# Attention followed by a gated FFN on one core: another instruction order, other engines for some steps, and e buffers handed out as they come free

## The chip, the core and the metric

The program runs on one NeuronCore of a Trainium2 chip. Times are microseconds of device time of one execution. Five engines matter: TensorE (PE) for matmuls and transpositions, VectorE (DVE), ScalarE (ACT) and GpSimd (POOL) for everything elementwise, and SyncE (SP), which issues the DMAs. Each engine runs its own instructions in order and waits on semaphores for the others.

## The reference

```python
for c in range(nc):                       # chunks of 32 queries
    q_c = q[:, :, c_start:c_end]          # context: 16 keys to the left, 8 to the right
    k_full = np.concatenate([mem_k, k_ctx], axis=2)      # 8 memory keys + context
    v_full = np.concatenate([mem_v, v_ctx], axis=2)
    scores = scale * np.matmul(q_c, k_full.transpose(0, 1, 3, 2))
    a = np.exp(scores - np.max(scores, axis=-1, keepdims=True))
    a = a / (np.sum(a, axis=-1, keepdims=True) + 1e-09)
    out[:, :, c_start:c_end] = np.matmul(a, v_full)
...
h = np.maximum(x @ w_in, 0.0)             # 512 -> 1024
conv_out = sum(conv_w[k] * hp[:, k:k+S] for k in range(3))   # depthwise over the sequence
gate = 1.0 / (1.0 + np.exp(-conv_out))
return h * gate @ w_out                   # 1024 -> 512
```

There are 4 batches, 8 heads of 64, 768 positions; x is the attention's output with the heads side by side (512 channels). q, k, v are float32; w_in, conv_w and w_out are float64 and come to the chip as pairs of 32-bit words.

## The kernel before

**Attention.** The work is cut into steps: one step is a pair of heads (128 rows of channels) and half of a sequence, 12 chunks of 32 queries. The first four steps stand alone, the others go two by two (GROUP). `scores` (L310, PE) writes a step's scores into the tile s, a pair of PSUM banks of which there is one. The softmax follows: a maximum (L267, DVE), then by the letter in SOFT either V, a subtraction out of s into the SBUF tile e (L269, DVE) and one exp over e (L270, ACT), or A, a scaling of the maxima (L272, DVE) and one exp for each group of 64 columns straight out of s (L283, ACT: 6 for a single step, 12 for a pair). Then come a memset at the sequence's ends (L286, L288), a sum (L290), a reciprocal (L293), and a multiplication (L294) on DVE or POOL by the letter in NORM. PE transposes e (L325) into the tile t, ACT copies it to w_t (L327), PE multiplies with v (L334, into t again), and t is split into a high part x_hi (L340, ACT) and the rest x_lo (L341, DVE), so that matmuls in fp32r keep the precision of float32. There are one t, one w_t and two e, and before the change e is handed out strictly in turn.

**Weights.** Each of 8 blocks of w_in and of w_out is loaded as 512 KB of words (L208; conv_w with L210) into one of four buffers and turned from float64 into a high and a low part by `from_f64` (L212 to L240): some ten elementwise operations, whose spread over DVE, ACT and POOL is set by a letter (C, M, R, S, r) in W_IN and W_OUT.

**FFN.** `ffn_in` multiplies x by one 128-column block of w_in, for half a sequence: four channel blocks, for each three matmuls (high by high, high by low, low by high; L358) into one of four PSUM banks f, then relu on ACT (L366). `gate` runs over a whole sequence: a first tap on ACT (L374) or DVE (L376) by TAP, two multiply-adds on DVE (L378), sigmoid on ACT (L379), a product (L381, DVE or POOL by MULT). `split` makes the high (L387, ACT) and the low part (L388, DVE or POOL by LO). `ffn_out` multiplies 128 positions by w_out: eight blocks of three matmuls (L402) into a bank f, a copy (L405, ACT), a DMA out (L406).

**Order.** The functions record some 1300 operations in a Plan; `Plan.run` emits them in the order of the table ORDER, which sets the order on each engine; semaphores follow from the data. The batches interleave: while PE does the FFN of one batch, the attention of the next is worked off between its matmuls. A tile is made at its first use; a ring of n tiles must have the tile n places back finished by then. The loads stand in the same order on SP, and an SP instruction that waits for a buffer holds back the loads behind it.

Of the kernel before, what the change touches and what calls it, by code (L numbers as in the profile page):

```python
# [24 lines left out]
W_IN, W_OUT = ('CSSRMSCr', 'CMCRRSRM')  # L25
TAP = 'AAAAAAAAVAVAVVVAVAVAVVAAVVAAVVAV'
MULT = 'VVVGVVGVVVVVGGGVGVVVVGVVVGGGVVVV'
LO = 'VVVVGGGVVVVVVVVVGVVVGVVVVGVVGVGV'
SOFT = 'VVVVVAAVVAVBVVVBVBVVVAVVVVAVVBAA'
NORM = 'GGVGGGVVGGGGGVGGVVGGVVVVVVVGVGVG'  # L30
# [71 lines left out]
class Plan:  # L102

    def __init__(self):
        self.ops, self.last, self.readers = ([], {}, defaultdict(list))
        self.rings, self.parts = ({}, defaultdict(list))
# [434 lines left out]
```

## Time and profile before

| | us |
|---|---|
| median of 3 runs (lowest, highest) | 353.03 (352.73, 353.37) |
| profiled execution | 352.37 |
| its span | 350.6 |
| PE busy in the span | 334.1 (95%) |
| DVE busy | 233.1 (66%) |
| ACT busy | 191.9 (55%) |
| POOL busy | 83.6 (24%) |
| end of the last matmul | 347.4 |

The span lasts from the first to the last instruction of the profiled execution; 1.77 us of that execution lie around it. PE's matmuls are pipelined, so the duration of one is longer than the distance to the next: for pace, the starts are to be compared. PE's instructions come to its queue in blocks by a DMA queue of their own (q8, "instruction": 35 packets, 0.57 MB in the whole span, for all engines), beside the loads (q1).

### The profile page before, as it was taken

The numbers are of one execution on the slowest core, as the hardware profiler recorded it, in microseconds if no ns is written. First come the engines' busy times: TensorE is split into PE (matmuls) and PEld (weight loads), VectorE is DVE, ScalarE is ACT, GpSimd is POOL, SyncE is SP. The second block draws the span as 40 slices with busy tenths as digits, with TensorE's granted clock in tenths as the row PEclk, the third lists the DMA queues.
The fourth block names the chain that finished last, engine by engine and source line by source line (L and its number), as shares of the span: only waits on it lengthen the run. The fifth ranks groups of instructions, "written<-read, shape, count | busy, mean of one in ns | idle before, by whom it ended". The sixth has DMA issues, their size and how long they took to land.

```text
span 350.6 us, 10290 instructions
## 1 busy us (share of the span) xinstructions
PE 334.1 (95%) x4536; PEld 297.1 (85%) x4536; DVE 233.1 (66%) x325; ACT 191.9 (55%) x314; POOL 83.6 (24%) x127
## 2 busy tenths in 40 slices
PE   1589999999999999999999999999999999999996
PEld 0468999989999998887888999998888988998885
DVE  4977998999989997989974143286840332678300
ACT  4434785877687869379842323456743352545311
POOL 1464245124473154111020000402200012121200
PEclk9999999999999999999999999999999999999999
DMA  7966979667677244022401600001212000100022
GB/s 261 391 216 204 314 249 333 230 208 228 200 206 251 66 154 148 27 93 75 125 20 36 243 0 32 0 2 60 65 45 93 30 1 2 60 0 2 0 105 76
DMA packets 19916, 42.49 MB, mean 121 GB/s; under 512 B 2336, under 2 KB 10784, under 8 KB 19872
## 3 DMA queue, kind: packets, MB, share of 16 engines
q1 hardware_dynamic: 19872, 41.85, 35.6%
q8 instruction: 35, 0.57, 0.7%
q14 instruction: 9, 0.07, 0.1%
HBM read 35.55 MB, written 6.29 MB: 119 GB/s over the span
## 4 chain that ended last, share of the span: by engine, by line
PE 85%; DVE 9%; DMA 3%; issue 1%; ACT 0%; POOL 0%; DVEq 0%; ACTq 0%; POOLq 0%
PE f L402 38%; PE f L358 34%; PE t L334 6%; PE s L310 4%; PE t L325 3%; DMA w<-in_w_out_dram 2%; DVE c L378 1%; DMA w<-in_w_in_dram 1%; DVE w_top L217 1%; DVE e L269 1%; DVE top L267 1%; DVE w_top L214 1%; DVE w L223 1%; DVE w_top L216 1%; DVE w L221 1%
## 5 line engine op out<-in xcount | busy, mean ns | idle before, releaser
L402 PE MATMUL f<-w_out_hi,g 128*128 128x512 f32 (+1 forms) x400 | 127.3, 387 | 0.0
L358 PE MATMUL f<-x_hi,w_in_hi 128*128 128x384 f32 x256 | 90.3, 353 | 0.0
L402 PEld LDWEIGHTS f<-w_out_hi,g 128*128 128x128 f32 x400 | 74.1, 188 | 15.2 <-ACT o_sb L405 0.2
L358 PE MATMUL f<-x_lo,w_in_hi 128*128 128x384 f32 x256 | 86.7, 339 | 0.0
L358 PE MATMUL f<-x_hi,w_in_lo 128*128 128x384 f32 x256 | 86.7, 339 | 0.0
L402 PE MATMUL f<-w_out_lo,g 128*128 128x512 f32 (+1 forms) x200 | 77.0, 385 | 0.0
L378 DVE SCALAR_TENSOR_TENSOR c<-h,cw,c 128x768 f32<-128x768 f32 x48 | 49.2, 1044 | 18.6 <-ACT c L374 17.4
L358 PEld LDWEIGHTS f<-x_hi,w_in_hi 128*128 128x128 f32 x256 | 48.6, 190 | 2.7 <-issue 0.2
L358 PEld LDWEIGHTS f<-x_hi,w_in_lo 128*128 128x128 f32 x256 | 48.8, 190 | 1.0
L358 PEld LDWEIGHTS f<-x_lo,w_in_hi 128*128 128x128 f32 x256 | 48.5, 190 | 0.0
L402 PEld LDWEIGHTS f<-w_out_lo,g 128*128 128x128 f32 x200 | 37.6, 188 | 6.6
L405 ACT COPY o_sb<-f 128x512 f32<-128x512 f32 (+1 forms) x25 | 14.2, 573 | 43.4 <-PE f L402 41.3
L379 ACT ACTIVATE c<-c 128x768 f32<-128x768 f32 x32 | 26.9, 847 | 19.6 <-DVE c L378 19.5
L366 ACT ACTIVATE h<-f 128x384 f32<-128x384 f32 x48 | 22.6, 490 | 26.3 <-PE f L358 26.3
L388 POOL TENSOR_TENSOR g<-c,g 128x768 fp32r<-128x768 f32 x8 | 15.4, 1925 | 70.9 <-PE f L402 35.2
L334 PEld LDWEIGHTS t<-w_t,v_t 64*64 64x64 f32 x1536 | 25.2, 140 | 4.6 <-issue 3.3
L334 PE MATMUL t<-w_t,v_t 64*64 64x32 f32 x1536 | 27.2, 224 | 0.1
L387 ACT CAST g<-c 128x768 fp32r<-128x768 f32 x24 | 19.8, 833 | 12.6 <-POOL c L381 7.1
L376 DVE TENSOR_SCALAR c<-h,cw 128x768 f32<-128x768 f32 x14 | 8.6, 617 | 26.3 <-ACT h L366 23.6
L388 DVE TENSOR_TENSOR g<-c,g 128x768 fp32r<-128x768 f32 x16 | 17.3, 1086 | 11.2 <-ACT g L387 11.0
L381 POOL TENSOR_TENSOR c<-c,h 128x768 f32<-128x768 f32 x5 | 8.9, 1781 | 63.4 <-ACT c L379 63.4
L341 DVE TENSOR_TENSOR x_lo<-t,x_hi 128x768 fp32r<-128x768 f32 (+1 forms) x18 | 15.5, 859 | 12.6 <-ACT x_hi L340 12.6
(68 smaller groups left out, 408.5 us busy)
## 6 DMA issues: line engine op xcount, KB each, us to landing
v_t<-in_v_dram SPq DMA_DIRECT2D x32, 384.0 KB, 4.4
k_t<-in_k_dram SPq DMA_DIRECT2D x28, 252.0 KB, 3.9
out_dram<-o_sb SPq DMA_DIRECT2D x23, 256.0 KB, 2.0
q_d<-in_q_dram SPq DMA_DIRECT2D x28, 192.0 KB, 4.4
w<-in_w_in_dram SPq DMA_DIRECT2D x8, 512.0 KB, 6.2
w<-in_w_out_dram SPq DMA_DIRECT2D x8, 512.0 KB, 5.3
h<-in_k_dram SPq DMA_DIRECT2D x4, 252.0 KB, 6.1
h<-in_q_dram SPq DMA_DIRECT2D x4, 192.0 KB, 5.8
```

The source lines that it names most:

```text
L310: nc.tensor.matmul(s.t[w * CH:(w + 1) * CH, h ^ w & 1, (i * NG + g) * KW:(i * NG + g + 1) * KW], lhsT=q_d.t[r, c], rhs=k_t.t[r, c * STEP:c ...
L325: nc.tensor.transpose(out=t.t[:, j, g * P:(g + 1) * P], in_=e.t[:, i, 1:1 + 2 * KW], identity=ident)
L334: nc.tensor.matmul(t.t[h * D:(h + 1) * D, c & 1, c // 2 * CH:(c // 2 + 1) * CH], lhsT=vs[i].t[r, o], rhs=w_t.t[r, i, o], start=True, stop= ...
L341: plan.op(lambda: nc.vector.tensor_tensor(out=lo(), in0=sums(), in1=hi().bitcast(F32), op=ALU.subtract), (t, *keys(x_hi)), keys(x_lo))
L358: nc.tensor.matmul(f.t[:, :TW], lhsT=w_in_p[c][:, fc, cc], rhs=x_p[a].t[:, cc], start=cc == 0 and i == 0, stop=cc == NCC - 1 and i == 2)
L366: nc.scalar.activation(h.t[:, 1 + o:1 + o + TW], f.t[:, :TW], AF.Relu)
L378: plan.op(lambda i=i: nc.vector.scalar_tensor_tensor(out=c.t, in0=h.t[:, i:i + S], scalar=w[i], in1=c.t, op0=ALU.mult, op1=ALU.add), (*H, ...
L379: plan.op(lambda: nc.scalar.activation(c.t, c.t, AF.Sigmoid), (c,), (c,))
L387: plan.op(lambda: nc.scalar.copy(out=g_hi(), in_=x()), (h,), (p[0],))
L388: plan.op(lambda: (nc.vector if lo == 'V' else nc.gpsimd).tensor_tensor(out=g_lo(), in0=x(), in1=g_hi().bitcast(F32), op=ALU.subtract), (h ...
L402: nc.tensor.matmul(ps.t[:, :n], lhsT=g[fc][a].t[:, tt * P:(tt + 1) * P], rhs=w_out_p[c][:, fc, o:o + n], start=fc == 0 and i == 0, stop=fc ...
L405: plan.op(lambda: nc.scalar.copy(out=o_sb.t[:, :n], in_=ps.t[:, :n]), (ps,), (o_sb,))
```

## The change

Three things change. The strings that set engines are other ones: of the first four steps' softmax letters, VVVV becomes AVAA; the w_in and w_out blocks have other conversion letters; TAP has 19 letters A in place of 18; SOFT as a whole has as many or more steps by A, and MULT, LO and NORM differ in places. ORDER is another permutation (of 1305 operations, since the kinds of conversion have different numbers of operations). And the rings are counted by tiles that are alive instead of by turn, with the two e buffers handed out from a list to which a finished tile's buffer returns. Lines behind the top of the file move by 3 (in `from_f64` by 4).

```diff
-W_IN, W_OUT = ('CSSRMSCr', 'CMCRRSRM')
-TAP = 'AAAAAAAAVAVAVVVAVAVAVVAAVVAAVVAV'
-MULT = 'VVVGVVGVVVVVGGGVGVVVVGVVVGGGVVVV'
-LO = 'VVVVGGGVVVVVVVVVGVVVGVVVVGVVGVGV'
-SOFT = 'VVVVVAAVVAVBVVVBVBVVVAVVVVAVVBAA'
-NORM = 'GGVGGGVVGGGGGVGGVVGGVVVVVVVGVGVG'
+W_IN, W_OUT = ('MSSSCSMR', 'SMCRSRSM')
+TAP = 'AAAAAAAAVVAVAAAAVAVAVVAVAAVVAVVV'
+MULT = 'GVVGVVGVGVVVGVGVVVVVGVVVGVGVVGGV'
+LO = 'VVGGVVGVGVVVGVVVVVVGVVVVGVGVVVGV'
+SOFT = 'AVAAVAVVAAABVVVBVBVVAAVVVVVVVBVA'
+NORM = 'GGVGGGGVVGGGGVVGGVGGGVGVGVVGGGVG'
 ORDER = (
-    64, 65, 1, 0, 3, 75, 17, 16, 85, 70, 33, 32, 66, 67, 18, 68, 69, 2, 71, 72, 73, 74, 4, 76, 190, 49, 5, 6, 19, 77,
+    64, 1, 0, 74, 16, 17, 84, 70, 65, 2, 71, 33, 32, 66, 67, 68, 69, 72, 48, 3, 73, 4, 136, 75, 5, 49, 6, 76, 34, 77,
...
-        self.rings, self.parts = ({}, defaultdict(list))
+        self.rings, self.parts, self.freed = ({}, defaultdict(list), {})
...
-                    assert len(used) < size or not used[-size].left, i
+                    assert sum((y.left > 0 for y in used)) < size, i
...
             do()
+            for x in tiles:
+                if not x.left and x.ring in self.freed:
+                    self.freed[x.ring].append(x.t)
             done.add(i)
...
+    plan.ring('e', len(e_of))
+    plan.freed['e'] = e_of
...
-        plan.ring('e', len(e_of))
-        e = Tile('e', lambda: e_of[len(plan.rings['e'][1]) % len(e_of)])
+        e = Tile('e', lambda: plan.freed['e'].pop(0))
```

**DVE at the first softmax.** L217 to L224 are conversions of the first w_in block, L267 and L269 the first step's softmax (tile s in, e_71 out), L286 to L293 the rest of it. Before:

```order
L223 SCALAR_TENSOR_TENSOR w_80<-w_80 128x512
L224 TENSOR_SCALAR w_80<-w_top 128x512
L267 TENSOR_REDUCE top<-s 128x2x3
L269 TENSOR_TENSOR e_71<-s,top 128x2x3x64
L214 TENSOR_SCALAR w_top<-w_top 128x512
L216 TENSOR_SCALAR w_top<-w_top 128x512
L286 MEMSET e_71 32x2x16
L290 TENSOR_REDUCE z<-e_71 128x6
L293 RECIPROCAL z<-z 128x6
```

After (all lines 3 or 4 higher, so L270 is the maximum):

```order
L228 TENSOR_SCALAR w_80<-w_top 128x512
L236 SCALAR_TENSOR_TENSOR w_in_lo<-w_80 128x512
L270 TENSOR_REDUCE top<-s 128x2x3
L275 TENSOR_SCALAR top<-top 128x6
L218 TENSOR_SCALAR w_top<-w_top 128x512
L220 TENSOR_SCALAR w_top<-w_top 128x512
L221 SCALAR_TENSOR_TENSOR w_top<-w_86,w_top 128x512
L289 MEMSET e_71 32x2x16
L293 TENSOR_REDUCE z<-e_71 128x6
```

One conversion more (L236) stands ahead of the maximum, a scaling (L275) takes the subtraction's place, and the exps that follow it stand on ACT (six of L286, straight out of s).

**PE when it begins with the FFN.** t_276 (t_285 after) is the values' tile of the second step, s_359 (s_378) the scores of the first pair of steps, f the FFN's banks. Before:

```order
L334 MATMUL t_276<-w_t_311,v_t_128 64x32 x24
L358 MATMUL f_346<-x_hi0_270,w_in_hi_75 128x384
L358 MATMUL f_346<-x_hi0_270,w_in_lo_76 128x384
L358 MATMUL f_346<-x_lo0_273,w_in_hi_75 128x384
L310 MATMUL s_359<-k_t_234,q_d_181 32x64 x24
L310 MATMUL s_359<-k_t_187,q_d_142 32x64 x24
L358 MATMUL f_411<-x_hi0_270,w_in_hi_75 128x384
L358 MATMUL f_411<-x_hi0_270,w_in_lo_76 128x384
```

After:

```order
L337 MATMUL t_285<-w_t_322,v_t_185 64x32 x24
L361 MATMUL f_365<-x_hi0_265,w_in_hi_75 128x384
L361 MATMUL f_365<-x_hi0_265,w_in_lo_76 128x384
L361 MATMUL f_365<-x_lo0_274,w_in_hi_75 128x384
L313 MATMUL s_378<-k_t_292,q_d_289 32x64 x24
L328 MATMUL t_409<-ident_66,e0_71 128x128 x3
L361 MATMUL f_416<-x_hi0_265,w_in_hi_75 128x384
L361 MATMUL f_416<-x_hi0_265,w_in_lo_76 128x384
L361 MATMUL f_416<-x_lo0_274,w_in_hi_75 128x384
L313 MATMUL s_378<-k_t_272,q_d_276 32x64 x24
L337 MATMUL t_409<-w_t_422,v_t_153 64x32 x24
```

Before, both halves of the pair's scores stand together after the first triple of FFN matmuls. After, a transposition and a triple stand between them.

**SP ahead of the first w_out block.** The names are the loads' buffers and sources, and brackets give the engines and queues for which SP waits. Before:

```order
L301 DMA k_t<-in_k_dram 128x504 [waits DMAHW5_49,DMAHW2_49,PE_49]
L301 DMA k_t<-in_k_dram 128x504 [waits DMAHW6_49,DMAHW3_49,PE_49]
L301 DMA q_d<-in_q_dram 128x384 [waits DMAHW4_49]
L208 DMA w_902<-in_w_out_dram 128x1024 [waits DVE_49]
L301 DMA q_d<-in_q_dram 128x384
L208 DMA w_999<-in_w_out_dram 128x1024 [waits DMAHW7_49,Pool_49]
L301 DMA v_t<-in_v_dram 128x768 [waits DMAHW0_49]
L208 DMA w_1003<-in_w_out_dram 128x1024 [waits DMAHW1_49,Activation_49,Pool_49]
```

After:

```order
L304 DMA v_t<-in_v_dram 128x768 [waits DMAHW2_49,PE_49]
L304 DMA q_d<-in_q_dram 128x384 [waits DMAHW5_49,DMAHW3_49,PE_49]
L304 DMA q_d<-in_q_dram 128x384 [waits DMAHW6_49,DMAHW4_49,PE_49]
L304 DMA k_t<-in_k_dram 128x504
L212 DMA w_904<-in_w_out_dram 128x1024 [waits Pool_49]
L212 DMA w_910<-in_w_out_dram 128x1024 [waits DMAHW7_49,Pool_49]
L304 DMA k_t<-in_k_dram 128x504 [waits DMAHW0_49]
```

The load of the first w_out block waits for DVE before, and for POOL after the change; the second one follows it directly.

## Rows read from the trace of the kernel before

**Rows 1.** Parts 1 and 4 of the page: busy us of each engine (share of the span, instructions), and the shares of the chain of work that ended last by engine.

```profile
PE 334.1 (95%) x4536; PEld 297.1 (85%) x4536; DVE 233.1 (66%) x325; ACT 191.9 (55%) x314; POOL 83.6 (24%) x127
...
PE 85%; DVE 9%; DMA 3%; issue 1%; ACT 0%; POOL 0%; DVEq 0%; ACTq 0%; POOLq 0%
```

**Rows 2.** The waits of PE: who was waited for, us in total, times, the longest. First in the window from 0 to 27 us, then, behind the dots, in the window from 27 to 347 us.

```profile
PE s L310 <- DMA h<-in_q_dram: 8.3, 2, 6.8
PE t L325 <- POOL e L294: 3.2, 2, 1.6
PE s L310 <- issue: 1.5, 1, 1.5
...
PE t L325 <- DVE x_lo L341: 0.2, 1, 0.2
```

**Rows 3.** The table of stretches: the stretch, its length, busy us of each engine (instructions), the granted clock of PE, the busy share of the DMA engines and GB/s.

```profile
10.00:20.00 10.00, 6.73 (x210) 5.11 (x197) 9.65 (x25) 4.34 (x9) 4.74 (x5) 1.00 1.03 394
20.00:30.00 10.00, 8.49 (x179) 7.20 (x175) 6.14 (x13) 3.56 (x8) 5.60 (x5) 1.00 0.62 192
30.00:71.00 41.00, 41.00 (x985) 37.76 (x983) 38.12 (x66) 29.19 (x57) 16.21 (x26) 1.00 0.79 263
```

**Rows 4.** The timeline of all engines at the end of the program: start, duration, engine, line and operation.

```profile
347.49 0.37 ACT L405 COPY o_sb<-f 128x256 f32<-128x256 f32 x1 [1.55 <-PE f L402]
```

**Rows 5.** The timeline of all engines, 7 to 12 us, the first softmax and the second scores; in brackets the idle time ahead and what ended it.

```profile
7.84 0.56 DVE L267 TENSOR_REDUCE top<-s 128x6 f32<-128x384 f32 x1
...
8.51 0.56 DVE L269 TENSOR_TENSOR e<-s,top 128x384 f32<-128x384 f32 x1
...
9.10 0.53 ACT L270 ACTIVATE e<-e 128x384 f32<-128x384 f32 x1 [0.39 <-DVE e L269]
...
9.30 0.96 PE L310 MATMUL s<-h 64*32 64x64 f32 x48 [1.50 <-DMA h<-in_q_dram]
...
11.65 0.33 SPq L301 DMA_DIRECT2D k_t<-in_k_dram  x1
...
11.90 0.47 PE L325 MATMUL t<-ident,e 128*128 128x128 f32 x1 [1.65 <-POOL e L294]
```

**Rows 6.** Groups by line and form in the window from 0 to 80 us, of DVE and, behind the last dots, of ACT: line, engine, operation, tiles, shapes, count, busy us, mean ns of one.

```profile
L232 DVE SCALAR_TENSOR_TENSOR w_in_lo<-w 128x512 fp32r<-128x512 uint32 x1 | 0.7, 703 | 0.0
...
L272 DVE TENSOR_SCALAR top<-top 128x12 f32<-128x12 f32 x1 | 0.2, 168 | 0.0
...
L283 ACT ACTIVATE e<-s,top 128x64 f32<-128x64 f32 x12 | 2.6, 346 | 0.0
```

**Rows 7.** The timeline of PE from 16.5 to 28.5 us.

```profile
16.83 0.91 PE L325 MATMUL t<-ident,e 128*128 128x128 f32 x3 [1.55 <-POOL e L294]
...
21.56 0.97 PE L310 MATMUL s<-k_t,q_d 64*32 64x64 f32 x48
24.04 0.96 PE L310 MATMUL s<-k_t,q_d 64*32 64x64 f32 x48 [1.51 <-issue]
...
25.41 0.52 PE L358 MATMUL f<-x_hi,w_in_lo 128*128 128x384 f32 x1
25.73 0.52 PE L358 MATMUL f<-x_lo,w_in_hi 128*128 128x384 f32 x1
...
27.96 0.34 PE L358 MATMUL f<-x_hi,w_in_lo 128*128 128x384 f32 x1
28.14 0.34 PE L358 MATMUL f<-x_lo,w_in_hi 128*128 128x384 f32 x1
```

**Rows 8.** The DMA queues in the window from 17 to 21.5 us and, behind the dots, from 21.5 to 22.8 us: packets, MB, share of the time of 16 engines.

```profile
q1 hardware_dynamic: 578, 1.61, 90.9%
...
q1 hardware_dynamic: 12, 0.03, 6.4%
q8 instruction: 1, 0.02, 5.3%
```

**Rows 9.** The timelines of DVE around 56 us and, behind the last dots, of PE around 71 us; the row of L217 reads the buffer into which the load of 56 us goes.

```profile
48.05 0.72 DVE L217 SCALAR_TENSOR_TENSOR w_top<-w,w_top 128x536 uint32<-128x536 uint32 x1
...
56.23 1.57 DVE L221 TENSOR_SCALAR w<-w 128x512 uint32<-128x512 uint32 x1 [1.27 <-DMA w<-in_w_out_dram]
...
71.33 0.85 PE L325 MATMUL t<-ident,e 128*128 128x128 f32 x6 [0.24 <-DVE x_lo L341]
```

**Rows 10.** Groups by line and form in the whole span: count, busy us, mean ns of one, and the idle time ahead of them.

```profile
L378 DVE SCALAR_TENSOR_TENSOR c<-h,cw,c 128x768 f32<-128x768 f32 x48 | 49.2, 1044 | 18.6 <-ACT c L374 17.4
...
L379 ACT ACTIVATE c<-c 128x768 f32<-128x768 f32 x32 | 26.9, 847 | 19.6 <-DVE c L378 19.5
...
L366 ACT ACTIVATE h<-f 128x384 f32<-128x384 f32 x48 | 22.6, 490 | 26.3 <-PE f L358 26.3
L387 ACT CAST g<-c 128x768 fp32r<-128x768 f32 x24 | 19.8, 833 | 12.6 <-POOL c L381 7.1 <-DVE c L381 4.4 <-PE f L402 0.7
...
L381 DVE TENSOR_TENSOR c<-c,h 128x768 f32<-128x768 f32 x11 | 10.4, 955 | 5.0 <-ACT c L379 5.0
...
L376 DVE TENSOR_SCALAR c<-h,cw 128x768 f32<-128x768 f32 x14 | 8.6, 617 | 26.3 <-ACT h L366 23.6 <-POOL h L348 1.8 <-POOL g L388 0.9
```

**Rows 11.** The timeline of PE in the last batch, matmuls of L402; the first row holds two of them.

```profile
330.17 0.63 PE L402 MATMUL f<-w_out_hi,g 128*128 128x512 f32 x2
330.63 0.39 PE L402 MATMUL f<-w_out_lo,g 128*128 128x512 f32 x1
```

117 rows, old and new, of the table ORDER are left out of this document.

## The prediction

> **What bounds the kernel now.** The reader should first take the page's busy shares and its chain of work. TensorE (PE) is busy 334.1 of 350.6 us, and the chain that ended last runs 85% through PE and 9% through VectorE (DVE) [rows 1]. So only two things can move the time: stretches in which PE has nothing to do, and stretches in which its matmuls run below full pace. The waits of PE say where the first are: 8.3 us for the first two loads, 3.2 us for the softmax ahead of the first two transpositions, 1.51 us put down to "issue", and then, from 27 to 347 us, one wait of 0.24 us [rows 2]. Everything between is gapless, and the work of PE is the same in both kernels (the same matmuls in another order). The table by stretches then shows who is near to holding PE up: from 10 to 20 us DVE is busy 9.65 of 10, and from 30 to 71 us 38.12 of 41 [rows 3]. The rest of the kernel has slack on every engine but PE. The last output's copy and its transfer follow PE's last matmul [rows 4], and both are the same in both kernels.
>
> I make the sum as differences. The profiled execution took 352.37 us (span 350.6 and 1.77 around it), 0.66 below the median of 353.03; a difference worked out against its span is put on the median.
>
> **First softmax, by ScalarE.** The change turns the first step's softmax from V to A. Before, the reduce starts at 7.84, the subtract at 8.51, the exp at 9.10, and the transposition at 11.90; the second step's scores run from 9.30, since the subtract had read the score bank by 9.07 and only a load kept them back [rows 5]. After, DVE has one more conversion op ahead of the reduce (L236, the L232 of before, 0.70 in the row) [rows 6]; I take 0.65 of it as delay, since the ops of DVE overlap a little, so the reduce comes near 8.5 and the scale (L275, the L272 of before, 0.17) near 9.1. Then ScalarE (ACT) runs six exps of 64 columns out of PSUM. Twelve of them cost 2.6 us together in the trace [rows 6], so six cost 1.3 and end near 10.6. From the end of the exp (9.63) to the transposition took 2.27 before [rows 5]: the transposition comes near 12.9, 1.0 us later. There is one pair of score banks, and the exps read it to the end, so the second scores start at 10.6 instead of 9.30, 1.3 us later, and what follows them (reduce, softmax, second transposition, which stood at 16.83) is late by as much. DVE has no hole between 10 and 20 us to catch up in [rows 3]; it saves a subtract of 0.56 [rows 5] at each of the A steps, and pays the scale. Term: PE's first matmul of L358 comes 1.2 us later (bounds 0.9 and 1.4).
>
> **The 1.51 us wait.** Before, PE stands still from 22.53 to 24.04 between two groups of scores, with no releaser in the records [rows 7]. From 17 to 21.5 us the loads keep 90.9% of the DMA engines' time and no packet of the instruction queue is served; in the 1.3 us after that, with the loads down to 6.4%, one is [rows 8]. I read it as PE's next block of instructions, fetched behind the loads. In the new order PE comes to the same count of instructions later by the 1.2 us of the first term and with a transposition group (t_409) and a matmul group ahead of it, so about 23.7. The packet should be there by then or within half a microsecond: the loads of this stage are the same and are issued no more than 1 us later. Term: -1.51 (bounds -1.5 and 0). Together with the first term: -0.3.
>
> The Trainium skill speaks against this reading. "DMA: Bandwidth & Descriptors", section Queues, rings and completion order, says that a DMA engine takes turns between queue rows packet by packet, so a fetch would not have to wait until the loads are drained, and "Runtime: NRT & Kernel Launch", section Instruction fetch mechanics, calls the cost of a block's refill mostly hidden. The trace has 4.5 us without such a packet under loads [rows 8], which is closer to my reading; by the Trainium skill's two pages the credit of 1.51 falls away, and the sum would be that of the second rival below.
>
> **Pace of PE.** Right after the wait the 128x384 matmuls last 0.52 us and start 0.32 apart, from 27.96 on 0.34 and 0.18, and the granted clock is given as 1.00 all through [rows 3, 7]. So some six matmuls and a transposition cost about 1.5 us more than at the later pace. The quick pace came 3.6 us after PE's last standstill ended. After the change, if PE runs without a standstill from about 20.1 on, the quick pace can come up to 1.5 us earlier in the work; with a short standstill at 23.7 it comes at the same work or later. Term: -0.5, a third of the way between 0 and -1.5, since a standstill of some tenths is likely.
>
> **The stage from 30 to 71 us.** Here the chain runs on DVE. It waits 1.27 us at 56.23 for the first w_out load, and 15 us on PE waits 0.24 for an x_lo of DVE [rows 9]. In the new order that load waits for POOL's conversion, no longer for a DVE op (L217) at 48.05; POOL is done with that buffer some 2 us earlier by my sum of row means (an estimate), so the 1.27 should go. In exchange DVE's conversions stand earlier against PE: adding the row means in both orders up to each transposition, DVE's deficit against PE is up to 0.7 us larger between 55 and 68 us. 0.24 - 1.27 + 0.7 is below zero, so the stall of 0.24 goes. One price is new: a later pair of steps gets its exps from ACT too, twelve of them (2.6 us) [rows 6] where a subtract of 0.96 freed the score banks; PE has f matmuls to run meanwhile, and I take 0.25 of a bound of 0.5. Term: 0.0 (bounds -0.24 and +0.9).
>
> **The rest.** From 71 us on PE waits for nobody in before [rows 2], and the new choices take some 5 us of row means off DVE ahead of the last batches and give about 7 to POOL, which is busy 83.6 of 350.6 [rows 1]. In the last batch the order is tighter: one channel block has 21 matmuls of L361 and 21 of L405 between its last f matmul and the first use of its g, at 0.18 and 0.23 us from start to start [rows 7, 11] 8.6 us; the smallest such distance before is 11.2. The chain that must fit is relu, tap, two multiply-adds, sigmoid, product, cast and subtract: 0.49 + 0.62 + 2 x 1.04 + 0.85 + 0.96 + 0.83 + 0.96 = 6.8, with the product's time for the subtraction of the same shape [rows 10]. It is hidden by 1.8 us unless DVE is two ops of about 1 us behind. Term: 0 (bounds 0 and +1). Freed e buffers and the changed assertion add no instruction: 0.
>
> **Sum.** +1.2 - 1.51 - 0.5 + 0 + 0 = -0.8; 353.03 - 0.8 = 352.2.
>
> **The rivals.** *The start is not bought back (slower).* The A softmax keeps the score banks, PE is 1.2 us late, and the block of instructions is late with it: the loads that the trace shows ahead of the packet [rows 8] also move by the same time, since they wait for the same buffers, so PE stands for about 1.5 us at t_409 or at the second half of the scores. Then +1.2, no credit, and pace unchanged or 0.3 worse: 354.2 to 354.5. It decides from 1.0 us of standstill between 20 and 26 us. For it speaks that loads wait on released buffers; against it that a load of k for this stage is issued by 11.65 already [rows 5]. *The standstill goes with the instruction count (slower).* The 1.51 falls where a block ends whatever the loads do, and is met again at that instruction: +1.2 and nothing back, 354.2. For it speaks that the row names no releaser [rows 7]; against it the missing packets under loads [rows 8]. *DVE takes the gain (no change).* The chain went through DVE from 40.56 to 71.2. If DVE, and not PE, sets the time there, what PE gains by 30 us is lost as a wait before 71, and only the 0.24 or a little of the 1.27 stays: 352.6 to 353.4, 352.9. For it speaks 38.12 of 41 us busy [rows 3]; against, that PE waited there just once. *The last batch runs dry.* The distance of 8.6 us is met by a chain of 6.8 and 2.7 of waiting in DVE's queue, 0.9 too late: 353.1 for one block, 354.0 if a second one follows so.
>
> **How the numbers follow.** Differences under 0.2%, 0.7 us, are about what a measurement of this kernel cannot tell from none: faster ends at 352.3, slower starts at 353.7. Chances: forecast 0.42, start not bought back 0.16, standstill by count 0.05, DVE takes the gain 0.30, last batch dry 0.07. The forecast's own range goes from -0.3 - 1.5 - 0.24 = -2.0 (351.0) to about -0.6; a tenth of it counts as the same, a tenth of the third rival as faster, and of the last 0.03 as the same. Faster 0.41, same 0.34, slower 0.25. The range goes from 351.0 to the 354.5 of the first rival.
>
> **What would show it.** Right: first transposition near 12.9 and scores of step 1 near 10.6; first L361 matmul near 21.5; no wait of PE above 0.7 us between 20 and 28 us; 0.18 us between 128x384 matmuls before 27 us; no DVE wait on a w_out load at 56 us; no PE wait from 28 us to its end, which comes near 346.6. Wrong: a PE wait of 1 us or more between 20 and 26 us (first rivals), waits for x_lo, e or w_t between 40 and 72 us (DVE takes the gain), or a wait of L405 for a g after 290 us. A first transposition at 12.0 would say that the A softmax costs nothing here.

## The result

Over 15 runs each the changed kernel took 355.37 us at the median, the kernel before 352.34; the ratio is 1.0087, with a 95% interval of 1.0066 to 1.0108. It is slower by about 3 us, and not faster by 0.8 as forecast. (The forecast started from 353.03, the median of three runs, 0.7 above that of the fifteen.) Its times also spread more: 352.85 to 360.28, against 351.02 to 353.37; three of them, 358.34, 358.79 and 360.28, count as slow and are left out of the ratio.

The profiled execution took 356.24 us, 3.9 more than that of the kernel before, and its span is 354.5 in place of 350.6. It is 0.9 above the median, so its waits add up to more than the median lost. The view of PE's waits, for the window from 0 to 352 us (who was waited for: us in total, times, longest), answers to [rows 2]:

```profile
PE s L313 <- DMA h<-in_q_dram: 6.2, 1, 6.2
PE s L313 <- DMA k_t<-in_k_dram: 3.7, 2, 2.1
PE s L313 <- ACT e L286: 3.3, 1, 3.3
PE t L328 <- POOL e L297: 2.8, 2, 1.7
PE t L337 <- DMA v_t<-in_v_dram: 1.0, 1, 1.0
PE t L337 <- issue: 0.3, 1, 0.3
```

The work of PE has not changed (334.0 us busy against 334.1 in [rows 1]). The first line is shorter than before. Lines 3 and 4 are the first softmax: the scores of the second step wait for the exps, the transpositions for the products. Lines 2 and 5 are new, 4.7 us of waiting for loads of k and v, and so is the last, 0.34 us without a releaser at 51.99. The timeline of PE shows where they stand; it answers to [rows 7] and goes on to 109 us:

```profile
20.58 0.69 PE L361 MATMUL f<-x_hi,w_in_hi 128*128 128x384 f32 x1
...
23.98 0.96 PE L313 MATMUL s<-k_t,q_d 64*32 64x64 f32 x48 [2.07 <-DMA k_t<-in_k_dram]
24.87 0.90 PE L328 MATMUL t<-ident,e 128*128 128x128 f32 x3
25.43 0.67 PE L361 MATMUL f<-x_hi,w_in_hi 128*128 128x384 f32 x1
...
28.67 0.44 PE L361 MATMUL f<-x_hi,w_in_hi 128*128 128x384 f32 x1
28.95 0.34 PE L361 MATMUL f<-x_hi,w_in_lo 128*128 128x384 f32 x1
...
40.04 1.25 PE L313 MATMUL s<-k_t,q_d 64*32 64x64 f32 x96 [1.64 <-DMA k_t<-in_k_dram]
...
108.25 1.60 PE L337 MATMUL t<-w_t,v_t 64*64 64x32 f32 x96 [0.99 <-DMA v_t<-in_v_dram]
```

The first matmul of L361 starts at 20.58, 0.28 later than at 20.30 before. Up to the last matmul, which starts at 350.99 in place of 347.12, 3.87 have been lost. So 3.6 of it is lost between. The waits there are 2.07 + 1.64 + 0.34 + 0.99 = 5.04, and were 1.51 + 0.24 = 1.75 [rows 2, 7]: 3.3 of the 3.6. Where the other 0.3 is lost isn't shown. The quick pace (matmuls of 0.34 us) begins at 28.95, 1.0 later than at 27.96, but 0.84 of that is already counted (0.28 for the first matmul, and 2.07 in place of 1.51), and the work done by then differs: 48 values' matmuls in place of three f matmuls.

Why k is late stands in SP's own timeline, 11 to 26 us:

```profile
11.06 0.33 SPq L212 DMA_DIRECT2D w<-in_w_in_dram  x1
15.76 0.33 SPq L304 DMA_DIRECT2D v_t<-in_v_dram  x1
16.14 1.13 SPq L304 DMA_DIRECT2D k_t<-in_k_dram  x1
17.32 0.90 SPq L304 DMA_DIRECT2D q_d<-in_q_dram  x2
18.26 0.43 SPq L304 DMA_DIRECT2D k_t<-in_k_dram  x1
```

For 4.4 us, from 11.4 to 15.8, SP issues nothing: the v load at 15.76 needs the buffer that PE's first values (L337, 14.20 to 15.70) free. The two k loads stand behind it, are issued at 16.14 and 18.26, and take 4.4 and 5.6 us to land; the second lands at 23.85, and PE starts its scores at 23.98. Before the change the first such k load went out at 11.65 [rows 5], the second at 13.66, both ahead of the v loads. The DMA engines meanwhile worked off what was queued and then stood idle, from about 16.1 to 16.6, as the view of the DMA queues from 16 to 18.6 us shows (40 slices, tenths busy, then GB/s and the loads' queue):

```profile
DMA  3000000000991992694999964999892924699621
GB/s 126 0 0 0 0 0 0 0 0 0 142 142 47 236 189 95 142 284 142 331 331 284 284 236 189 425 378 473 331 567 95 362 95 189 109 203 155 93 31 31
q1 hardware_dynamic: 171, 0.44, 66.6%
```

Later nothing is lost to waiting: from 127 to 316 us PE is busy in every microsecond of both traces. The table of stretches of the changed kernel (the first two columns of engines are PE and its weight loads, then DVE, ACT, POOL; [rows 3] has the first of these stretches):

```profile
30.00:71.00 41.00, 39.02 (x972) 35.94 (x972) 34.16 (x65) 30.05 (x66) 14.35 (x26) 1.00 0.79 263
71.00:127.00 56.00, 55.01 (x1201) 52.02 (x1200) 47.86 (x72) 45.17 (x75) 30.99 (x36) 1.00 0.59 192
127.00:191.00 64.00, 64.00 (x741) 53.15 (x741) 53.97 (x63) 41.56 (x55) 16.42 (x11) 1.00 0.29 92
191.00:316.00 125.00, 125.00 (x997) 113.67 (x996) 57.89 (x62) 55.49 (x84) 13.33 (x40) 1.00 0.11 38
```

The last two of these stretches before the change:

```profile
127.00:191.00 64.00, 64.00 (x736) 52.38 (x735) 53.38 (x69) 43.32 (x64) 12.35 (x15) 1.00 0.22 73
191.00:316.00 125.00, 125.00 (x1002) 114.09 (x1001) 56.08 (x64) 56.59 (x96) 15.81 (x32) 1.00 0.13 45
```

DVE has become less busy in the stretch from 30 to 71 us, 34.16 in place of 38.12, and yet PE loses 1.98 there.

### The profile page after: what moved, and what is told of

Read it like the earlier page. It is cut to its first block, busy times and chain, and to the rows that moved or that the text cites. A ratio compares the mean times of both kernels' runs of the same rounds, so it can differ in the third digit from the quotient of the medians.

```text
span 354.5 us, 10325 instructions
## 1 busy us (share of the span) xinstructions
PE 334.0 (94%) x4536; PEld 297.5 (84%) x4536; DVE 226.4 (64%) x321; ACT 196.3 (55%) x328; POOL 90.7 (26%) x130
## 4 chain that ended last, share of the span: by engine, by line
PE 90%; DMA 5%; DVE 2%; SPq 1%; issue 0%; POOL 0%; ACT 0%; POOLq 0%; DVEq 0%; ACTq 0%
PE f L405 38%; PE f L361 37%; PE t L337 7%; PE s L313 5%; DMA k_t<-in_k_dram 3%; PE t L328 3%; DMA v_t<-in_v_dram 1%; DMA w<-in_w_in_dram 1%; SPq L304 1%; DVE w_top L221 0%; DVE w_top L220 0%; POOL e L297 0%; DVE w L227 0%; DVE w_in_lo L236 0%; DVE w_top L218 0%
## 5 line engine op out<-in xcount | busy, mean ns | idle before, releaser
L405 PE MATMUL f<-w_out_hi,g 128*128 128x512 f32 (+1 forms) x400 | 128.9, 388 | 0.0
L361 PE MATMUL f<-x_hi,w_in_hi 128*128 128x384 f32 x256 | 89.6, 350 | 0.0
L361 PE MATMUL f<-x_lo,w_in_hi 128*128 128x384 f32 x256 | 86.6, 338 | 0.0
L361 PE MATMUL f<-x_hi,w_in_lo 128*128 128x384 f32 x256 | 86.6, 338 | 0.0
L361 PEld LDWEIGHTS f<-x_hi,w_in_hi 128*128 128x128 f32 x256 | 48.3, 189 | 2.5
L361 PEld LDWEIGHTS f<-x_hi,w_in_lo 128*128 128x128 f32 x256 | 48.4, 189 | 1.5
L361 PEld LDWEIGHTS f<-x_lo,w_in_hi 128*128 128x128 f32 x256 | 48.4, 189 | 0.0
L369 ACT ACTIVATE h<-f 128x384 f32<-128x384 f32 x48 | 23.1, 492 | 44.1 <-PE f L361 43.8
L337 PEld LDWEIGHTS t<-w_t,v_t 64*64 64x64 f32 x1536 | 25.6, 141 | 5.7 <-issue 3.2
L297 POOL TENSOR_TENSOR e<-e,z 128x768 f32<-128x768 f32 (+1 forms) x13 | 18.5, 1419 | 43.6 <-DVE z L296 39.5
L337 PE MATMUL t<-w_t,v_t 64*64 64x32 f32 x1536 | 27.7, 226 | 1.3 <-DMA v_t<-in_v_dram 1.0
L330 ACT COPY w_t<-t 128x768 f32<-128x768 f32 (+1 forms) x18 | 13.1, 726 | 19.1 <-PE t L328 19.1
L313 PEld LDWEIGHTS s<-k_t,q_d 64*32 64x32 f32 x1344 | 15.6, 108 | 8.0 <-issue 7.3
```

Of the source, the lines that this page charges most:

```text
L297: plan.op(lambda: (nc.vector if norm == 'V' else nc.gpsimd).tensor_tensor(out=keep()[:, :N], in0=keep()[:, :N], in1=z.t[:, :N].unsqueeze(3 ...
L313: nc.tensor.matmul(s.t[w * CH:(w + 1) * CH, h ^ w & 1, (i * NG + g) * KW:(i * NG + g + 1) * KW], lhsT=q_d.t[r, c], rhs=k_t.t[r, c * STEP:c ...
L330: plan.op(lambda: nc.scalar.copy(out=w_t.t[:, :ns].rearrange('p i c q -> p i (c q)'), in_=t.t[:, :ns, :NG * P]), (t,), (w_t,))
L337: nc.tensor.matmul(t.t[h * D:(h + 1) * D, c & 1, c // 2 * CH:(c // 2 + 1) * CH], lhsT=vs[i].t[r, o], rhs=w_t.t[r, i, o], start=True, stop= ...
L361: nc.tensor.matmul(f.t[:, :TW], lhsT=w_in_p[c][:, fc, cc], rhs=x_p[a].t[:, cc], start=cc == 0 and i == 0, stop=cc == NCC - 1 and i == 2)
L369: nc.scalar.activation(h.t[:, 1 + o:1 + o + TW], f.t[:, :TW], AF.Relu)
```

## The experiments

Theory 1: loads are late because SP issues in order, and the new order puts loads that wait for PE ahead of loads that PE needs next. Theory 2: the DMA engines are full there, and the order of the loads does not matter. Theory 3: the first softmax on ACT costs the time at the start.

**k_first.** The changed kernel; two k loads and two q loads go ahead of the waiting v load in ORDER, which on SP reads

```diff
 L212 DMA w_193<-in_w_in_dram 128x1024 [waits DMAHW7_49,DVE_49]
-L304 DMA v_t<-in_v_dram 128x768 [waits DMAHW0_49,PE_49]
-L304 DMA k_t<-in_k_dram 128x504 [waits DMAHW1_49]
-L304 DMA q_d<-in_q_dram 128x384 [waits DMAHW2_49]
+L304 DMA k_t<-in_k_dram 128x504 [waits DMAHW0_49]
+L304 DMA q_d<-in_q_dram 128x384 [waits DMAHW1_49]
+L304 DMA k_t<-in_k_dram 128x504 [waits DMAHW2_49]
 L304 DMA q_d<-in_q_dram 128x384 [waits DMAHW3_49]
-L304 DMA k_t<-in_k_dram 128x504 [waits DMAHW4_49]
+L304 DMA v_t<-in_v_dram 128x768 [waits DMAHW4_49,PE_49]
```

> The changed kernel, with one edit: the two k loads and two q loads for the first pair of steps are issued on SP ahead of the fourth v load, which waits for PE's values. Theory 1, issue order: PE's wait of 2.07 us at 23.98 was for loads that stood on SP behind that v load; they are then issued near 11.5 to 13 us, the wait goes, and the kernel is 1.5 to 2.1 us faster than the changed one (ratio to the kernel before about 1.003). Theory 2, bandwidth: the DMA engines are 84% busy there, so other loads arrive later by as much; less than 0.5 us comes back. Theory 3, first softmax on ScalarE: it sets the start, and no load order gives anything (ratio 1.009).

Measured: 353.61 at the median, ratio to the kernel before 1.0054 (1.0028 to 1.0080). The changed kernel had 1.0087, so about 1.2 us came back; that is more than theory 2 allows and less than theory 1 asked, and since the two intervals overlap the ratio alone doesn't decide. PE's waits in the window from 20 to 352 us say what became of the rest:

```profile
PE t L337 <- DMA v_t<-in_v_dram: 1.4, 2, 0.8
PE s L313 <- issue: 1.4, 1, 1.4
PE s L313 <- DVE w_top L221: 0.3, 1, 0.3
```

The wait of 2.07 for k is gone, and of the 1.64 some 0.34 is left, at 35.86 (the last line: the profile names a DVE operation, but these are the scores that waited at 40.04, and their k load landed at 35.62). Two waits for v loads (1.4 together, where one of 0.99 was) and a standstill without a releaser, 1.37 us at 38.43, have come in their place.

**three_waits.** The same, and the two later load waits are taken away too: in ORDER, operations 155 and 156 (f matmuls) and 275 go ahead of 271 (the scores that waited at 40.04), and 685 (the v load for 108 us) goes ahead of 748 (a k load that waits for PE).

```diff
-    ... 271, 120, 113, 112, 275, 293, ... 155, ... 156, ...
+    ... 155, 156, 275, 271, 120, 113, 112, 293, ...
...
-    ... 748, 959, 698, 731, 685, 747, ...
+    ... 685, 748, 959, 698, 731, 747, ...
```

> The edit of the run before, and two more for the two other load waits of PE: two triples of f matmuls stand ahead of the scores that waited 1.64 us at 40.04 (and the two halves of these scores change places), and the v load that PE waited 0.99 us for at 108 is issued ahead of a k load that waits for PE. Theory 1: all three waits go, 4 to 4.7 us less than the changed kernel, so 0.3 to 1 us below the kernel before (ratio 0.997 to 1.000). Theory 2: at most 1.5 us less. Theory 3: no change.

Measured: 353.09, ratio 1.0028 (1.0005 to 1.0051). The interval lies wholly under that of the changed kernel: two thirds of the loss are gone, 2.1 us by the ratios, and in the profiled execution (span 350.5, against 350.6 before) all waits for k and v with them. (That execution, 352.26, is the quickest of its twelve.)

```profile
PE s L313 <- DMA h<-in_q_dram: 6.1, 1, 6.1
PE s L313 <- ACT e L286: 4.4, 2, 3.5
PE t L328 <- POOL e L297: 2.8, 2, 1.7
PE s L313 <- issue: 0.4, 1, 0.4
```

That is more than the 1.5 of theory 2, and less than theory 1 asked, which saw the kernel before beaten. 0.28% is left. In this trace PE waits mostly for the exps on ACT, 3.45 us at the start and 0.98 at 43.78. The edits for 40 and 108 us were not run one by one, and the intervals of k_first and three_waits overlap, so what each of them gives isn't shown.

**soft_v.** The changed kernel with the first four softmax letters as before.

```diff
-SOFT = 'AVAAVAVVAAABVVVBVBVVAAVVVVVVVBVA'
+SOFT = 'VVVVVAVVAAABVVVBVBVVAAVVVVVVVBVA'
```

> The changed kernel with the first four steps' softmax by V again, order unchanged. Theory 3: the A softmax cost the start 1.2 us and more, so 1 to 3 us come back. Theory 1: PE comes to the second scores up to 1 us earlier, but the late k loads still end at 23.8 or a little earlier, since their issue waits for the first step's values; 0 to 1 us comes back. Theory 2: no change within 0.3 us.

Measured: 357.02, ratio 1.0109 (1.0064 to 1.0154). No gain shows; with six runs the interval leaves room for 0.8 us at most, and theory 3 asked for 1 to 3. The first f matmul comes at 20.78, no earlier than 20.58. The profiled execution, the longest (360.61), still waits 1.20 us at 23.31 for k, and 2.01 at 42.02, where the profile names a w_in load but a k load had landed just before, at 41.78. Behind the second wait the granted clock stood at the lower level (1.2 GHz, mean 0.50) from 43.25 to 50.08, which lengthens this execution; the four runs with a mean clock above 0.995 have a median of 355.5, still not below the changed kernel. Theory 3 falls as an account of the difference between the two kernels.

**before_soft_a.** The same letters in the other direction, in the kernel before.

```diff
-SOFT = 'VVVVVAAVVAVBVVVBVBVVVAVVVVAVVBAA'
+SOFT = 'AVAAVAAVVAVBVVVBVBVVVAVVVVAVVBAA'
```

> The kernel before with the first four steps' softmax letters AVAA, order unchanged. Theory 3: 1 to 3 us slower (ratio 1.003 to 1.009). Theory 1: the k loads there are issued by 13.7 us, so only the later scores count: 0.3 to 1.2 us slower, less what the wait of 1.51 us at 24.04 takes up (ratio 1.000 to 1.003). Theory 2: no change.

Measured: 354.60, ratio 1.0070 (1.0039 to 1.0100), more than theory 1 allowed and within theory 3. PE's waits from 8 to 352 us:

```profile
PE s L310 <- ACT e L283: 5.1, 2, 3.3
PE t L325 <- DVE x_lo L341: 3.0, 1, 3.0
PE t L325 <- POOL e L294: 0.9, 1, 0.9
PE s L310 <- DMA k_t<-in_k_dram: 0.8, 1, 0.8
```

With ACT and DVE in the old order, the second transposition waits 3.0 us behind an x_lo (second line), and of the first line's 5.1 us 1.8 are a wait of the first pair's scores for exps. So the letters and the order belong together. The A softmax costs 2.5 us (0.70%) in an order made for V, while taking it out of the order that was made for it shows no gain.

**before_k_late.** The other half of theory 1: the kernel before gets the fault alone. Its two k loads are issued behind the v load that waits for PE.

```diff
-L301 DMA k_t<-in_k_dram 128x504 [waits DMAHW0_49]
-L208 DMA w_228<-in_w_in_dram 128x1024 [waits DMAHW1_49]
-L301 DMA k_t<-in_k_dram 128x504 [waits DMAHW2_49]
-L301 DMA v_t<-in_v_dram 128x768 [waits DMAHW3_49]
-L301 DMA v_t<-in_v_dram 128x768 [waits DMAHW4_49,PE_49]
+L208 DMA w_226<-in_w_in_dram 128x1024 [waits DMAHW0_49]
+L301 DMA v_t<-in_v_dram 128x768 [waits DMAHW1_49]
+L301 DMA v_t<-in_v_dram 128x768 [waits DMAHW2_49,PE_49]
+L301 DMA k_t<-in_k_dram 128x504 [waits DMAHW3_49]
+L301 DMA k_t<-in_k_dram 128x504 [waits DMAHW4_49]
```

> The kernel before, with one edit: the two k loads for the first pair of steps are issued behind the v load that waits for PE's values, as in the changed kernel (near 15.5 us in place of 11.65 and 13.66). Theory 1, issue order: PE waits for k_t at about 22 us for 0.5 to 2 us; this partly stands in the place of the 1.51 us at 24.04, so 0.3 to 2 us slower (ratio 1.001 to 1.006). Theory 2, bandwidth: the same bytes pass in the same time, no more than 0.3 us either way.

Measured: 353.24, ratio 1.0046 (1.0020 to 1.0071), inside theory 1's range. The trace has the new wait at the expected place, 0.73 us at 22.25 for k_t, and one of 0.86 at 32.34; the standstill of 1.51 is gone. Its profiled execution is its quickest (351.80), so the trace does not show the whole of the 0.46%.

**before_w_late.** A test of the prediction's reading of the 1.51 us in the kernel before: 512 KB are taken out of the loads of that stage.

```diff
 L301 DMA v_t<-in_v_dram 128x768 [waits DMAHW4_49,PE_49]
-L208 DMA w_353<-in_w_in_dram 128x1024 [waits DMAHW5_49,Pool_49]
-L301 DMA k_t<-in_k_dram 128x504 [waits DMAHW6_49,DMAHW2_49,PE_49]
+L301 DMA k_t<-in_k_dram 128x504 [waits DMAHW5_49,DMAHW2_49,PE_49]
+L208 DMA w_415<-in_w_in_dram 128x1024 [waits DMAHW6_49,Pool_49]
```

> The kernel before, with one edit: the load of a w_in block (512 KB, issued at 15.77 us) is issued behind the next k load, which waits for PE until 22.5. Fetch theory: the instruction packet, which came at 21.60 as the loads drained, comes earlier by 1 us or more, and PE's wait of 1.51 us ending at 24.04 shrinks under 0.5; 0.5 to 1.5 us faster unless the conversion of this block is then late. Rival, the wait goes with the instruction count: it stays at 1.5 and no time is gained.

Measured: 350.61, ratio 0.9964 (0.9946 to 0.9983): faster than the kernel before, and the only version here that beats both kernels. The DMA queues in its window from 19 to 20.3 us:

```profile
q1 hardware_dynamic: 98, 0.25, 49.0%
q8 instruction: 1, 0.02, 5.2%
```

The instruction packet is served here, and not from 21.5 on as in [rows 8]. PE passes the place without a standstill: scores, 96 matmuls in one row, then f at the quick pace from 23.08, 4.9 us earlier than in [rows 7], with six f matmuls and a transposition fewer done:

```profile
20.80 0.52 PE L358 MATMUL f<-x_lo,w_in_hi 128*128 128x384 f32 x1
21.25 1.62 PE L310 MATMUL s<-k_t,q_d 64*32 64x64 f32 x96
22.80 0.44 PE L358 MATMUL f<-x_hi,w_in_hi 128*128 128x384 f32 x1
23.08 0.34 PE L358 MATMUL f<-x_hi,w_in_lo 128*128 128x384 f32 x1
```

So the reading held: with 512 KB fewer ahead of it the packet started at 19.10 in place of 21.60, and the standstill went. No late load had caused it: the k loads issued at 11.65 and 13.66 had landed by 19.77, the q loads before them. The expected gain was 0.5 to 1.5; it is 1.3. It is not the standstill alone: the quick pace came earlier too, and other waits took a part back (0.65 for x_hi at 28.36, 0.52 for k at 31.30, 0.40 without a releaser at 78.15). So theory 2 has a part of the truth: how much is queued counts too, and not only in which order.

**three_waits_v8.** three_waits, with the pair of steps at 41 us by V.

```diff
-SOFT = 'AVAAVAVVAAABVVVBVBVVAAVVVVVVVBVA'
+SOFT = 'AVAAVAVVVAABVVVBVBVVAAVVVVVVVBVA'
```

> The kernel of three_waits with the softmax of the pair of steps at 41 us by V in place of A, since PE waited 0.98 us at 43.78 for its twelve exps. If that wait is worth its length: 0.7 to 1 us less than three_waits (ratio to before 1.000). If DVE, which gets a subtract of 0.96 us, is late for something else instead: no change or slower.

Measured: 353.86, ratio 1.0050 (1.0025 to 1.0075); no gain. The wait of 0.98 went, and other ones came (0.89 for ACT's relu at 41.95, 1.16 for v at 50.67).

**after_again, after_third, after_fourth.** The changed kernel as it is, three more single executions.

> The changed kernel once more, to see which of its waits vary from run to run. Issue order: waits for k_t near 24 and 40 us and for v_t near 108 us come again, with lengths that differ by up to 1 us; the rest of PE's waits after 30 us stays at zero.

> The changed kernel a third time, one look. If loads and instruction packets that land at other moments make its spread: PE's waits between 20 and 55 us differ again from the two looks so far (5.0 and 1.6 us in total after the first f matmul and up to 71 us), and a standstill of over 1 us may be followed by a stretch at a granted clock of 0.5. If the spread has another cause: the same waits as in the first look within 0.3 us each.

> The changed kernel a fourth time, one look, for the same question as the run before: other waits between 20 and 55 us if landing times make the spread, the same waits if not.

Measured: 355.07, 353.40 and 355.18. The v load of 108 us was waited for in all four executions (0.99, 0.69, 0.83, 0.36), a k load near 22 to 24 us or at 32 to 40 us in each of them, but with other lengths: 2.07 and 1.64 in the first; 0.38 at 32.16, and none at 22, in the second; 0.46 and 0.86 in the third; 1.95 at 23.75 and 0.86 in the fourth. (For the 1.95 the profile names a DVE operation; but the same scores wait there as in the first execution, and the later k load landed at 23.61, just ahead of them, as there.) What was expected of after_again failed in part: no wait near 24 us, and a standstill of 1.26 at 33.97. So the waits vary with the moments at which the loads land. The second execution adds a loss that no wait shows. Its timeline of PE from 33 to 39 us:

```profile
33.97 0.34 PE L313 MATMUL s<-k_t,q_d 64*32 64x64 f32 x13 [1.26 <-issue]
...
34.68 0.34 PE L361 MATMUL f<-x_lo,w_in_hi 128*128 128x384 f32 x1
...
35.04 0.53 PE L361 MATMUL f<-x_hi,w_in_lo 128*128 128x384 f32 x1
35.36 0.53 PE L361 MATMUL f<-x_lo,w_in_hi 128*128 128x384 f32 x1
...
37.28 0.53 PE L361 MATMUL f<-x_lo,w_in_hi 128*128 128x384 f32 x1
37.60 1.23 PE L328 MATMUL t<-ident,e 128*128 128x128 f32 x6
38.58 0.42 PE L361 MATMUL f<-x_hi,w_in_hi 128*128 128x384 f32 x1
```

After 1.26 us of standstill the matmuls last 0.53 in place of 0.34, and start 0.32 apart in place of 0.17, up to 38.6. Its table of stretches gives the granted clock of it (third from the end):

```profile
34.00:38.00 4.00, 4.00 (x27) 3.82 (x28) 3.51 (x6) 0.00 (x0) 0.46 (x1) 0.63 0.69 217
```

0.63 is the mean of the stretch: full speed up to 35.0, and behind it the lower of the two levels (1.2 GHz), which lasts to 38.4. Eight starts 0.15 farther apart and a group of transpositions that takes 0.98 in place of 0.57 make 1.6 us: more than the standstill itself. The record has the mean granted clock of every execution, and the 3.4 us of this fall show there as 0.994. A mean of 0.990 to 0.995 stands beside 3 of the 15 runs of the changed kernel (358.10, 358.79 and 360.28 us), 3 of 12 of k_first, 2 of 12 of three_waits, 2 of 6 of soft_v, 1 of 9 of before_soft_a and 1 of 8 of three_waits_v8, and beside none of the 47 runs of the kernel before that were taken along with these, nor of before_k_late and before_w_late. So such falls are a part of the wider spread, but hardly of the slower median: without those three runs it is still 355.1. Not every standstill brings one: there was none behind the 1.37 of k_first or the 1.95 of the fourth execution.

**The rings and the e buffers alone.** With the old tables the new ring count and the list of freed e buffers give the same instructions with the same waits on every engine, so this part of the change has no time of its own. This was read from the two programs; there is no run of it.

## Why the prediction was wrong

**What bounds the kernel** was right: PE sets the end, its work is unchanged, and only standstills and pace moved the time. From 127 to 316 us PE waits for nothing in either trace.

**First softmax, 1.2 us later (0.9 to 1.4): mis-sized.** The second scores came at 10.43 (forecast 10.6), but the first transposition at 12.46, 0.56 later than before and not 1.0, and the first f matmul only 0.28 later. The timeline of all engines, 4 to 13 us, of the changed kernel, and behind the last dots one row of the kernel before:

```profile
7.57 0.69 DVE L236 SCALAR_TENSOR_TENSOR w_in_lo<-w 128x512 fp32r<-128x512 uint32 x1
8.18 0.55 DVE L270 TENSOR_REDUCE top<-s 128x6 f32<-128x384 f32 x1
...
9.04 1.34 ACT L286 ACTIVATE e<-s,top 128x64 f32<-128x64 f32 x6 [0.73 <-DVE top L275]
...
10.43 0.97 PE L313 MATMUL s<-h 64*32 64x64 f32 x48 [3.31 <-ACT e L286]
...
11.44 0.56 DVE L270 TENSOR_REDUCE top<-s 128x6 f32<-128x384 f32 x1
...
10.80 0.52 DVE L267 TENSOR_REDUCE top<-s 128x6 f32<-128x384 f32 x1
```

The exps were sized rightly (1.34 for six). The first reduce came 0.34 later and not 0.65, with L236 ahead of it as foreseen. And what follows the second scores is not late by as much as they are: they came 1.13 later, but the second reduce (last two rows) only 0.64, since DVE was at work on conversions and on the first step's sum until then in both kernels. The first load, which landed at 6.16 in place of 6.84, has no part in this: in the four executions of the changed kernel it landed between 6.16 and 6.93, and the first f matmul came at 20.47 to 20.70, later than before by 0.17 to 0.40.

**The 1.51 us: this step failed.** The prediction gave the credit because "the loads of this stage are the same and are issued no more than 1 us later". They were the same, but were issued 4.5 us later, behind a v load that waits for PE. I had read the order of DVE and PE at this place, and that of SP only at the w_out blocks. The standstill of 1.51 was indeed gone, but a wait of 2.07 for k stood in its place, and k_first shows that without that wait a standstill comes up later, 1.37 at 38.43. The mechanism of the term, a fetch held up by loads, was right, as before_w_late shows; the second rival, a standstill that goes with the instruction count whatever the loads do, is out: taking 512 KB of loads away brought the packet from the window of 21.5 to 22.8 into that of 19 to 20.3, and the standstill went. The Trainium skill ("DMA: Bandwidth & Descriptors", Queues, rings and completion order) has the DMA engines take turns between queues packet by packet. The traces agree in part: in the kernel before, an instruction packet was served from 15.78 to 16.84, while the loads took 95.9% of the engines' time; but from 16.3 to 19 us in before_w_late, with the loads taking all of their time (102.4% by the view), none was. What had been asked for by then, the traces don't show.

**Pace, -0.5: did not come.** It was made to depend on little or no standstill at 23.7; with 2.07 there, the quick pace came 1.0 later. before_w_late shows the other end of the term: without a standstill it came at 23.08.

**30 to 71 us, 0.0 (-0.24 to +0.9): failed in kind.** DVE was the engine looked at, and it got lighter by 4 us; the wait on the w_out load at 56 and the 0.24 at 71 went. The loss came from a k load again, 1.64 at 40.04, issued at 35.01 when the scores before it had freed its buffer. The rival "DVE takes the gain" had the place and not the cause.

**The rest, 0 (0 to +1).** No wait in the last batch, as forecast. The 0.99 for v at 108 us was in no term.

**The rivals.** "The start is not bought back" came nearest: its mark, over 1.0 us of standstill between 20 and 26 us, was met, but by a wait for k and not by a late block of instructions, and PE was 0.84 later there (0.28, and 2.07 in place of 1.51) where the rival had 1.2. What lay beyond the range was the sum of three load waits, where it had one standstill. Its own argument, "loads wait on released buffers", was the right one to follow further.

Still open: the 0.28% by which three_waits is slower than the kernel before. Softmax waits at the start and at 43.78 are the candidates in its trace, but soft_v and three_waits_v8 gave nothing, so no cause is shown. Falls of the clock don't account for it either: without the two runs with a mean clock of 0.995, its slowest, the median is 353.0.

## What to carry to other kernels

Where one engine issues all loads in order, read its order first, with what each load waits for, and note which loads stand behind a wait for the engine that will need them. A load that waits for a buffer belongs behind those whose buffers are free. A reorder table that makes the elementwise engines lighter can lose on this queue what it gains, and a burst of loads can hold up the instructions of the engine for which it is meant; moving one load of 512 KB by one place on SP gave 1.3 us here. The choice of engines counts with the order it was made for: four softmax letters put into another order cost 2.5 us.

## What the runs showed of the hardware

The standstills without a releaser ended 1.3 to 1.5 us after the end of a packet of the instruction queue that came in a burst of loads or just behind one: in the kernel before the packet ends at 22.69 and PE goes on at 24.04; in k_first it lies between 36.2 and 37.3 us and PE goes on at 38.43; in the second execution of the changed kernel it lies between 31.5 and 32.6 and PE goes on at 33.97. In k_first the loads had 97.5% of the engines' time from 33.5 to 36.2, with no such packet.

Where they stand goes by the count of PE's instructions. Counted in the traces (matmuls and weight loads), 449, 705, 1217 (three times), 1473, 1985 and 3265 instructions lie ahead of the eight standstills of over 0.2 us that name no releaser, in seven traces: each number is 193 more than a multiple of 256. No wait of PE for a named releaser stands at such a count. Whether PE stands there goes by the packet: at 705 the kernel before stood for 1.51 us, before_w_late and the changed kernel not at all.

And the page's clock can read 1.00 while the matmuls stand 0.32 us apart (from the first f matmul to the quick pace, which begins between 23.1 and 33.2 us by the trace), so that pace is to be read from the starts of the matmuls; later, in the second execution, the same 0.32 came with a granted clock that had fallen.
